# Late heads: the load of turned probabilities moves from SyncE's queue to ScalarE's, and the load of queries and keys moves behind the store

## The chip, the cores and the metric

The kernel runs on one core of one Trainium2 chip. The metric is the device time of one execution in microseconds (us). The time before is the median of three executions.

## The reference

The reference is causal attention with a forgetting gate on 4 x 8 heads, 576 positions and 64 features per head, followed by two pairs of dense layers on 2304 tokens:

```
scores = q @ k.T / 8 + cum[:, None] - cum[None, :]     # cum = cumsum(log f), causal mask
attn   = exp(scores - rowmax) / rowsum;  x = attn @ v   # heads side by side: [2304, 512]
h = relu(x @ w_in);   x = (h * h) @ w_out              # 512 -> 2048 -> 512
h = x @ w2_in;  y = (h - tanh(h)) @ w2_out             # 512 -> 2048 -> 512
```

All of it is float32. The kernel computes a float32 product from rounded halves: each operand is split into a rounded part and a rest, and three products are summed.

## The kernel before, in words

**Three kinds of work on one TensorE.** The attention of the 32 heads and the first dense pair run interleaved. The first pair (phase 1) works on eight blocks of 288 tokens. For each block and each of 16 slices `i` of the 2048 hidden units, `h_step` makes 12 matmuls (tile `hp`, line 138), ScalarE applies relu and the square (lines 148 to 150), an engine makes the rest `gl` (line 101), and two slices later `y_step` makes 12 matmuls (tile `yp`, line 164). In the stretch spoken of here `hp` has a single PSUM bank, so the next 12 `hp` matmuls wait until ScalarE's relu (line 148) has read the bank. The second pair (phase 2) follows when all heads are done. PSUM banks for attention come from one pool of three.

**Heads 16 to 31, the late heads.** `attention_late` handles head `k` in five steps. `scores(k, t)` makes the five score tiles: matmuls into `s_ps` (lines 476, 477), row minimum on VectorE (443), exponential on ScalarE (452), normalisation (463). `turn(t)` transposes the tile in 32 x 32 pieces on VectorE into the single tile `T` (lines 503, 506, 509). When all five are turned, `put(k)` stores `T` (1 MB) to memory (`p_d<-T`, line 512), and `get(k)` loads it back in four pieces in an order that completes the transposition (`PTl<-p_d`, line 518). `PTl` and `PTh` are single tiles. `split_p` makes the rounded half `PTh` on GpSimd (recorded at line 90 of a helper) and the rest `PTl` on VectorE (line 101), in four chunks. `pv(k)` multiplies with the values (tile `o_ps`, lines 549, 552, 554); its first matmul needs the first chunk of `PTh`. The result's upper half is evicted from PSUM by ScalarE as `xt` (the call of `rounded` in `pv`, recorded at line 88), and VectorE adds it to the lower half. Every second head stores the pair's output (`x_d<-xsh`, `x_d<-xs`).

Since `PTl` is a single tile, `get(k)` has to wait until the last matmul of `pv(k-1)` has read it, and it has to wait until the store `put(k)` has landed. In the program `get(k)` stands at the end of the step, behind `pv(k-1)`.

`load(k+2)` loads the queries and keys of the head after next into the single tile `R` (576 KB, line 225) and four rows into `QB` (line 227); `prep` splits `R` into `QA` and `QB` on ScalarE, VectorE and GpSimd one step later. In the program `load(k+2)` stands ahead of the second half of `split_p`.

**Who issues and in which order.** Before, SyncE's queue issues all loads and stores (`ENG["put"]` and `ENG["get"]` are `"S"`). An engine runs its instructions in a fixed order, and an instruction that waits holds up all behind it. The first two blocks keep the order of the program text. From the third block on a list scheduler places the instructions of every engine by its own estimates of time, within the dependencies. `tc.issue_after(ins)` adds one: what is issued inside it on the engine of `ins` comes behind `ins`. So a small change in the text gives another order on all engines.

In the rows and the text a head's load is called early when the head's last turn stands, in VectorE's order, ahead of the split of the head before; it is called late when that turn stands behind the split.

Of the kernel before, what the change touches and what calls it, by code (L numbers as in the profile page):

```python
# [16 lines left out]
B, H, S, D = 4, 8, 576, 64  # L17
NU = B * H
# [15 lines left out]
ENDS = (28, 27, 27, 27, 32, 24)  # L34
ENG = {
# [18 lines left out]
def kernel(  # L54
# [25 lines left out]
    def pre(u):  # L80
        return "" if u < UT else "l_"

    def by(name):
        return {"A": nc.scalar, "V": nc.vector, "P": nc.gpsimd, "S": nc.sync}[ENG[name]]

    def rounded(eng, out, in_):
        if eng is nc.scalar:
            eng.activation(out, in_, AF.Copy)  # L88
        elif eng is nc.gpsimd:
            eng.tensor_scalar(out, in_, 1.0, 1.0, ALU.mult, ALU.mult)  # L90
        else:
            eng.tensor_copy(out, in_)
# [80 lines left out]
    psa = att.enter_context(tc.tile_pool(name="psa", bufs=3, space=bass.MemoryType.PSUM))  # L173

    STORED = set()
    R, QA, QB, VR, VH, ST, XS, P, PT = {}, {}, {}, {}, {}, {}, {}, {}, {}

    def latest(engine):
        return next(x for x in reversed(nc.cur_bb.bb.instructions) if x.engine == engine)
# [43 lines left out]
    def load(u):  # L223
        R[u] = one.tile([128, 2, S], F32, tag="R", name="R")
        nc.sync.dma_start(R[u], qk[u])
        QB[u] = two.tile([68, 2, S], F32R, tag="QB", name="QB")
        nc.sync.dma_start(QB[u][64:68].bitcast(F32), aug_d[u])
# [7 lines left out]
    def prep(u):  # L235
        r = R.pop(u)
        qa = two.tile([128, 2, S], F32R, tag="QA", name="QA")
        QA[u] = qa
        split_qk(r, qa, QB[u], *(pre(u) + x for x in ("qb_q", "qa_lo", "qb_lo")))
        ST[u] = two.tile([128, 4, 6], F32, tag="ST", name="ST")  # L240
        by(pre(u) + "st").memset(ST[u], 1.0)

    def load_v(u):
        VR[u] = two.tile([128, 5, D], F32, tag="VR", bufs=2, name="VR")
        nc.sync.dma_start(VR[u], v[u])
# [183 lines left out]
    def store_x(b, pair, xs, c0, c1):  # L429
        STORED.add((b, pair, c1))  # L430
        n = c1 - c0
        xh = one.tile([128, S], F32R, tag="xsh", name="xsh")
        rounded(by(pre(b * H) + "xh"), xh[:, :n], xs[:, c0:c1])
        rest(by(pre(b * H) + "xl"), xs[:, c0:c1], xs[:, c0:c1], xh[:, :n])
        nc.sync.dma_start(x_d[b][pair][:, 0, c0:c1], xh[:, :n].bitcast(F32))
        nc.sync.dma_start(x_d[b][pair][:, 1, c0:c1], xs[:, c0:c1])
# [28 lines left out]
    def bank(u, name):  # L465
        return psa.tile([128, 512], F32, tag="at", name=name)

    def scores(u, t):
        qa, qb, st = QA[u], QB[u], ST[u]
        n, q0 = NKEY[t], Q0[t]  # L470
        rows = 64 if t == 0 else 128
        cuts = [(0, 320), (320, 576)] if t == 4 else [(0, n)]
        mn = None
        for i, (a, b) in enumerate(cuts):
            ps = bank(u, "s_ps")
            nc.tensor.matmul(ps[:, :b - a], qa[:, 0, q0:q0 + 128], qa[:, 1, a:b], start=True, stop=False)  # L476
            nc.tensor.matmul(ps[:, :b - a], qb[:, 0, q0:q0 + 128], qb[:, 1, a:b], start=False, stop=True)  # L477
            mn = row_min(P[t], ps, st, t, i, a, b, mn)
        soften(P[t], st, t, mn, f"{pre(u)}n{t}")
# [20 lines left out]
    def turn(t):  # L500
        p, T = P[t], PT["t"]
        if t == 0:
            nc.vector.transpose(T[0:64, 0:2, 3, 0], p[0:64, :64].rearrange("p (b j) -> p b j", b=2))
            return
        nch = min(t + 1, 4)
        nc.vector.transpose(T[:, :, :nch, t - 1].rearrange("p b a j -> p a b j"),
                            p[:, :nch * 128].rearrange("p (a b j) -> p a b j", a=nch, b=4))
        if t == 4:
            nc.vector.transpose(T[:, 0:2, 2, 0], p[:, 512:576].rearrange("p (b j) -> p b j", b=2))

    def put(u):
        by("put").dma_start(p_d[u % 2], PT["t"].rearrange("p b a s j -> p (b a s j)"))

    def get(u):
        src = p_d[u % 2].rearrange("(q i) (b n) -> i q b n", q=4, b=4)
        for b in range(4):
            dst = PT["l"][32 * b:32 * b + 32].rearrange("p q a s j -> p q (a s j)")
            by("get").dma_start(dst.bitcast(F32), src[:, :, b])  # L518
# [8 lines left out]
    def pv(u):  # L527
        vh, vr = VH.pop(u), VR.pop(u)
        b, h = divmod(u, H)
        e = h % 2  # L530
        ps = bank(u, "o_ps")
        if u < UT:
            hi, lo = (PT[k].rearrange("p q a s j -> p (q a s j)").rearrange("p (c t j) -> p c t j", c=4, t=4) for k in "hl")
            po = ps.rearrange("p (s j) -> p s j", s=4)
            at = lambda p, c, t: p[:, c, t:]
            po4, p4 = ps[0:64, 384:512].rearrange("p (q j) -> p q j", q=4), PT["t"][0:64, :, 3, 1]
            po_at = lambda t: po[:, t:]
            p0 = PT["t"][0:64, 2:4, 3, 0]
        else:
            hi, lo = PT["h"], PT["l"]  # L540
            po = ps.rearrange("p (q s j) -> p q s j", q=4, s=4)
            at = lambda p, c, t: p[:, :, c, t:]
            po4, p4 = po[0:64, :, 3], lo[0:64, :, 2, 0].bitcast(F32)
            po_at = lambda t: po[:, :, t:]
            p0 = lo[0:64, 0:2, 3, 0].bitcast(F32)
        seq = [(hi, 0), (hi, 1), (lo, 1), (hi, 2), (lo, 2), (hi, 3), (lo, 3), (None, 4), (lo, 0)]
        for n, (pt, c) in enumerate(seq):
            if pt is None:
                nc.tensor.matmul(po4, vr[0:64, 4], p4, start=False, stop=False)
                continue  # L550
            t = max(0, c - 1)
            nc.tensor.matmul(po_at(t), vh[:, c].rearrange("p a d -> p (a d)"), at(pt, c, t), start=(n == 0), stop=(n == 8))  # L552
        ps0 = bank(u, "o0_ps")
        nc.tensor.matmul(ps0[0:64, 0:64], vr[0:64, 0], p0, start=True, stop=True)
        if e == 0:
            XS[0] = two.tile([128, S], F32, tag="xs", name="xs")
        xs = XS[0]
        r = slice(64 * e, 64 * e + 64)
        xt = one.tile([64, 512], F32, tag="xsh", name="xt")
        rounded(nc.scalar, xt, ps[64:128])  # L560
        if u < UT:
            nc.vector.tensor_tensor(xs[r, 64:], ps[0:64], xt, ALU.add)
        else:
            nc.vector.tensor_tensor(
                xs[r, 64:].rearrange("p (s q j) -> p q s j", s=4, q=4),
                ps[0:64].rearrange("p (q s j) -> p q s j", q=4, s=4),
                xt.rearrange("p (q s j) -> p q s j", q=4, s=4), ALU.add,
            )
        rounded(by(pre(u) + "xs0"), xs[r, 0:64], ps0[0:64, 0:64])
        if e == 1:  # L570
            store_x(b, h // 2, xs, 0, S)
# [42 lines left out]
    def attention_late():  # L614
        for k in range(UT + 1, NU + 1):
            now = k < NU
            if now:
                load_v(k)
                scores(k, 4)
            yield  # L620
            if now:
                scores(k, 3)
                turn(4)
            yield
            if k + 1 < NU:
                prep(k + 1)
            prep_v(k - 1)
            split_p(0)
            if now:
                scores(k, 2)  # L630
                turn(3)
            yield
            if k + 2 < NU:
                load(k + 2)
            split_p(1)
            if now:
                scores(k, 1)
                scores(k, 0)
                turn(2)
            yield  # L640
            if now:
                turn(1)
                turn(0)
                put(k)
            pv(k - 1)
            yield
            if now:
                get(k)

    X = {0: [f1.tile([128, NK, TB], F32R, tag="xhl", bufs=4, name="xhl") for _ in range(2)]}  # L650
    setup()
# [221 lines left out]
```

## Time and profile before

| | |
|---|---|
| median of 3 executions | 1088.86 us (1084.09 to 1089.58) |
| profiled execution | 1081.43 us, span 1079.7 us |
| mean granted TensorE clock | 0.987 |
| TensorE busy | 1029.2 us, 95% of the span |
| VectorE, ScalarE, GpSimd busy | 594.0, 524.7, 250.6 us |
| DMA | 134.83 MB, 38.9% of the engines' span on one queue |
| late heads, from the first store to the last output | about 255 to 550 us of the span |

TensorE is PE in the rows, its weight loads are PEld, VectorE is DVE, ScalarE is ACT, GpSimd is POOL, SyncE is SP; a q behind the name (SPq) is the engine's queue of issued transfers. A row with `[2.17 <-POOL PTh L90]` says that the engine sat idle for 2.17 us before the instruction and that the split on GpSimd ended this. The granted clock is the share of TensorE's full 2.4 GHz; the lower level is 1.2 GHz.

### The profile page before, as it was taken

Reading aid. Unit: us, or ns where it says so; the run is one execution under the profiler, and the core shown is the slowest. Engines: PE = TensorE matmul, PEld = TensorE weight load, DVE = VectorE, ACT = ScalarE, POOL = GpSimd, SP = SyncE. Lnnn points to the kernel's source line nnn. Section 1 sums busy time; section 2 is a strip of 40 time slices with the busy share of each in tenths; the row PEclk is TensorE's granted clock in tenths of the full one; section 3 lists DMA queues with packets and bytes.
Section 4 is the critical chain, followed back from the end, with each engine's and each line's share of the span. In section 5 each row is a group of like instructions: output and inputs, shape, how many; then the busy total and the mean of one; then the engine's idle time right before and its main releaser. Section 6 shows DMA issues by size and latency. Waiting matters only on the chain.

```text
span 1079.7 us, 16821 instructions
## 1 busy us (share of the span) xinstructions
PE 1029.2 (95%) x6048; PEld 898.8 (83%) x6048; DVE 594.0 (55%) x1566; ACT 524.7 (49%) x1221; POOL 250.6 (23%) x358
## 2 busy tenths in 40 slices
PE   4899999999999898999999999999999999999998
PEld 3577678888998888888889999888888888888898
DVE  5887777768787767877525545642222322222232
ACT  6977677665556446455436667432222222222232
POOL 4244455555353442534210000000000000000000
PEclk9989999999999899999989999999999999999999
DMA  7657643225955658745646088100200300110010
GB/s 243 199 138 213 185 140 136 89 82 174 293 180 171 195 154 253 258 141 162 184 161 228 2 305 285 45 1 25 92 1 1 117 1 1 39 40 1 1 40 21
DMA packets 63301, 134.83 MB, mean 125 GB/s; under 512 B 6416, under 2 KB 31568, under 8 KB 61168
## 3 DMA queue, kind: packets, MB, share of 16 engines
q1 hardware_dynamic: 63216, 133.74, 38.9%
q8 instruction: 48, 0.79, 0.3%
q14 instruction: 37, 0.30, 0.1%
HBM read 93.94 MB, written 39.78 MB: 124 GB/s over the span
## 4 chain that ended last, share of the span: by engine, by line
PE 75%; DMA 11%; DVE 6%; POOL 2%; issue 2%; SPq 2%; ACT 2%; POOLq 0%; ACTq 0%; DVEq 0%
PE hp L138 32%; PE yp L164 32%; DMA PTl<-p_d 6%; PE o_ps L552 3%; DMA p_d<-T 3%; PE o_ps L367 2%; DVE PTl L101 2%; PE s_ps L476 1%; SPq L518 1%; DVE P L443 1%; PE s_ps L477 1%; DMA raw<-in_w_dram 1%; POOL PTh L90 1%; PE s_ps L326 1%; PE t_ps L487 1%
## 5 line engine op out<-in xcount | busy, mean ns | idle before, releaser
L138 PE MATMUL hp<-xhl,w 128*128 128x288 f32 (+2 forms) x2496 | 454.2, 329 | 2.5 <-ACT tmp L148 1.7
L138 PEld LDWEIGHTS hp<-xhl,w 128*128 128x128 f32 x2496 | 388.8, 192 | 41.0 <-issue 2.7
L164 PE MATMUL yp<-ghl,w 128*128 128x512 f32 (+1 forms) x960 | 216.0, 374 | 0.0
L164 PE MATMUL yp<-gh,w 128*128 128x288 f32 x1024 | 200.9, 301 | 0.0
L164 PEld LDWEIGHTS yp<-ghl,w 128*128 128x128 f32 x960 | 168.4, 188 | 34.5
L153 DVE TENSOR_TENSOR tmp<-hp,tmp 128x512 f32<-128x512 f32 (+1 forms) x80 | 51.0, 638 | 209.8 <-ACT tmp L152 209.8
L164 PEld LDWEIGHTS yp<-gh,w 128*128 128x128 f32 x1024 | 161.9, 191 | 1.6 <-issue 0.4
L152 ACT ACTIVATE tmp<-hp 128x512 f32<-128x512 f32 (+1 forms) x80 | 44.4, 555 | 225.0 <-PE hp L138 224.8
L164 PE MATMUL yp<-gl,w 128*128 128x288 f32 x512 | 133.5, 299 | 2.6 <-DVE gl L101 1.5
L148 ACT ACTIVATE tmp<-hp 128x288 f32<-128x288 f32 x128 | 51.9, 407 | 121.6 <-PE hp L138 118.4
L452 ACT ACTIVATE P<-P,ST 128x320 f32<-128x320 f32 (+4 forms) x151 | 84.6, 561 | 39.5 <-DVE ST L443 38.2
L164 PEld LDWEIGHTS yp<-gl,w 128*128 128x128 f32 x512 | 90.4, 190 | 5.0 <-DVE gl L101 2.3
L463 POOL TENSOR_SCALAR P<-P,ST 128x448 f32<-128x448 f32 (+4 forms) x88 | 58.4, 666 | 93.3 <-DVE ST L457 52.3
L101 DVE TENSOR_TENSOR ghl<-tmp,ghl 128x512 fp32r<-128x512 f32 (+1 forms) x80 | 51.1, 639 | 49.2 <-ACT ghl L88 49.2
L443 DVE CUSTOM_DVE_ANT_0 P<-s_ps,mk 128x320 f32<-128x320 f32 (+3 forms) x151 | 63.6, 433 | 25.2 <-PE s_ps L477 12.0
L101 DVE TENSOR_TENSOR gl<-tmp,gh 128x288 fp32r<-128x288 f32 x96 | 48.4, 505 | 47.2 <-ACT tmp L150 46.6
L101 DVE TENSOR_TENSOR PTl<-PTl,PTh 128x512 fp32r<-128x512 f32 (+1 forms) x64 | 51.9, 841 | 39.4 <-POOL PTh L90 39.3
L88 ACT ACTIVATE ghl<-tmp 128x512 fp32r<-128x512 f32 (+1 forms) x80 | 47.2, 590 | 49.9 <-DVE tmp L153 49.8
L101 DVE TENSOR_TENSOR w<-wst,w 128x512 fp32r<-128x512 f32 x64 | 46.1, 725 | 28.9 <-ACT w L88 28.6
L90 POOL TENSOR_SCALAR PTh<-PTl 128x512 fp32r<-128x512 f32 (+1 forms) x64 | 46.3, 750 | 59.8 <-DMA PTl<-p_d 59.0
L149 ACT ACTIVATE gh<-tmp 128x288 fp32r<-128x288 f32 x128 | 56.5, 443 | 4.1 <-PE yp L164 1.2
L150 ACT ACTIVATE tmp<-tmp 128x288 f32<-128x288 f32 x128 | 56.0, 438 | 2.1
(122 smaller groups left out, 1187.7 us busy)
## 6 DMA issues: line engine op xcount, KB each, us to landing
raw<-in_w_dram SPq DMA_DIRECT2D x64, 512.0 KB
p_d<-T SPq DMA_DIRECT2D x16, 1024.0 KB
PTl<-p_d SPq DMA_DIRECT2D x64, 256.0 KB
R<-in_qk_dram SPq DMA_DIRECT2D x24, 576.0 KB
xhl<-y_d SPq DMA_DIRECT2D x16, 512.0 KB
xhl<-x_d SPq DMA_DIRECT2D x14, 576.0 KB
y_d<-yst SPq DMA_DIRECT2D x14, 576.0 KB
VR<-in_v_dram SPq DMA_DIRECT2D x32, 160.0 KB
```

The source lines that it names most:

```text
L88: eng.activation(out, in_, AF.Copy)
L90: eng.tensor_scalar(out, in_, 1.0, 1.0, ALU.mult, ALU.mult)
L101: eng.tensor_tensor(out, in_, hi.bitcast(F32), ALU.subtract)
L138: nc.tensor.matmul(ps, w[:, k * 128:(k + 1) * 128], xk, start=(jj == 0), stop=(jj == 11))
L148: nc.scalar.activation(tmp, ps, AF.Relu)
L149: nc.scalar.activation(gh, tmp, AF.Square)
L150: nc.scalar.activation(tmp, tmp, AF.Square)
L153: nc.vector.tensor_tensor(tmp, ps, tmp, ALU.subtract)
L164: nc.tensor.matmul(yp[m][:, :n], w[:, c], x, start=(i == 0 and j == 0), stop=(i == NF - 1 and j == 2))
L443: nc.vector.tensor_tensor_reduce(p[:rows, a:b], ps[:rows, :b - a], mk[:rows, o:o + b - a], -0.125, 3.0e38 if mn is None else mn, ALU.add, ...
L452: nc.scalar.activation(p[:rows, :n], p[:rows, :n], AF.Exp, bias=mn, scale=-1.0, accum_out=st[:rows, 1, t:t + 1])
L463: by(n_by).tensor_scalar(p[:rows, :n], p[:rows, :n], st[:rows, 3, t:t + 1], 1.0, ALU.mult, ALU.mult)
```

## The change

`get` is issued from ScalarE. In `attention_late` it is issued within the step, behind the eviction `xt` of `pv(k-1)`, which the new dictionary `XT` remembers. `load(k+2)` moves from ahead of `split_p(1)` to behind `put(k)`, and is tied behind it on SyncE. The load of head 16, which stands in `attention`, changes its engine alone.

```diff
-    "w1_lo0": "V", "w1_lo1": "V", "w2_lo0": "V", "w2_lo1": "V", "sq": "V", "w1_sh": "V", "w2_sh": "V", "gl7": "V", "put": "S", "get": "S", "xld": "S", "wld": "S", "gl": "P", "qb_q": "A", "qa_lo": "V", "qb_lo": "P", "vh": "V", "vl": "V",
+    "w1_lo0": "V", "w1_lo1": "V", "w2_lo0": "V", "w2_lo1": "V", "sq": "V", "w1_sh": "V", "w2_sh": "V", "gl7": "V", "put": "S", "get": "A", "xld": "S", "wld": "S", "gl": "P", "qb_q": "A", "qa_lo": "V", "qb_lo": "P", "vh": "V", "vl": "V",
@@ -558,6 +558,7 @@
         xt = one.tile([64, 512], F32, tag="xsh", name="xt")
         rounded(nc.scalar, xt, ps[64:128])
+        XT[0] = latest(EngineType.Activation)
@@ -630,8 +631,6 @@
             yield
-            if k + 2 < NU:
-                load(k + 2)
             split_p(1)
@@ -642,10 +641,14 @@
                 put(k)
+                if k + 2 < NU:
+                    with tc.issue_after(latest(EngineType.SP)):
+                        load(k + 2)
             pv(k - 1)
+            if now:
+                with tc.issue_after(XT[0]):
+                    get(k)
             yield
-            if now:
-                get(k)
```

**The load's place.** On SyncE before, from the store of head 25 (`p_d_72`) to the load of head 26 (`p_d_71`); the pieces of `get` stand behind the store and behind `VR`, the values of a later head:

```order
L512 DMA p_d_72<-T 128x2048
L245 DMA VR<-in_v_dram 128x320
L518 DMA PTl<-p_d_72 32x4x512 x4
L227 DMA QB<-aug_d 4x1152
L713 DMA y_d<-yst 128x4x288 x2
L737 DMA xhl<-x_d_69 128x4x288
L225 DMA R<-in_qk_dram 128x1152
L737 DMA xhl<-x_d_69 128x4x288
L245 DMA VR<-in_v_dram 128x320
L512 DMA p_d_71<-T 128x2048
L435 DMA x_d_70<-xsh 128x576
L436 DMA x_d_70<-xs 128x576
```

On SyncE now, the same two stores:

```order
L512 DMA p_d_72<-T 128x2048
L225 DMA R<-in_qk_dram 128x1152
L227 DMA QB<-aug_d 4x1152
L245 DMA VR<-in_v_dram 128x320
L716 DMA y_d<-yst 128x4x288 x2
L740 DMA xhl<-x_d_69 128x4x288 x2
L245 DMA VR<-in_v_dram 128x320
L512 DMA p_d_71<-T 128x2048
L225 DMA R<-in_qk_dram 128x1152
L227 DMA QB<-aug_d 4x1152
```

On ScalarE now, behind the eviction of head 25's output, with the late load of head 26; `QA<-R` is the first step of `prep`:

```order
L88 ACTIVATE xt<-o_ps 64x512
L88 ACTIVATE VH<-VR 128x4x64
L88 ACTIVATE xsh<-xs 128x576
L148 ACTIVATE tmp<-hp 128x288
L149 ACTIVATE gh<-tmp 128x288
L150 ACTIVATE tmp<-tmp 128x288
L452 ACTIVATE P_1553,ST<-P_1553,ST 128x576
L452 ACTIVATE P_1551,ST<-P_1551,ST 128x448
L518 DMA PTl<-p_d_71 32x4x512 x2
L148 ACTIVATE tmp<-hp 128x288
L518 DMA PTl<-p_d_71 32x4x512
L149 ACTIVATE gh<-tmp 128x288
```

SyncE no longer issues the pieces; the store is followed at once by `R`. On ScalarE a late load stands several instructions behind the eviction. An early load, as that of head 25, stands directly behind it:

```order
L88 ACTIVATE QA<-R 128x1152
L88 ACTIVATE xt<-o_ps 64x512
L518 DMA PTl<-p_d_72 32x4x512 x4
L148 ACTIVATE tmp<-hp 128x288
L452 ACTIVATE P_1553,ST<-P_1553,ST 128x576
L452 ACTIVATE P_1551,ST<-P_1551,ST 128x448
```

So a wait of these four pieces holds up the relu (line 148) and the exponentials (452) behind them.

**VectorE around the split of head 19.** Before, the last turn of head 20 (`T<-P_1547`) stands behind the four chunks of the split (`PTl<-PTl,PTh`):

```order
L503 STREAM_TRANSPOSE T<-P_1546 64x2x32
L101 TENSOR_TENSOR gl<-tmp,gh 128x288
L101 TENSOR_TENSOR PTl<-PTl,PTh 128x4x128 x2
L101 TENSOR_TENSOR PTl<-PTl,PTh 128x4x96
L101 TENSOR_TENSOR PTl<-PTl,PTh 128x4x64
L506 STREAM_TRANSPOSE T<-P_1547 128x2x4x32
```

Now:

```order
L503 STREAM_TRANSPOSE T<-P_1546 64x2x32
L101 TENSOR_TENSOR gl<-tmp,gh 128x288
L506 STREAM_TRANSPOSE T<-P_1547 128x2x4x32
L101 TENSOR_TENSOR PTl<-PTl,PTh 128x4x128 x2
L101 TENSOR_TENSOR PTl<-PTl,PTh 128x4x96
L101 TENSOR_TENSOR gl<-tmp,gh 128x288
```

The last turn of head 20, and with it the store, moved ahead of the split of head 19.

**TensorE between the output of head 24 and that of head 25.** Before, from the last matmul of head 24's output to the first of head 25's there are 40 matmuls of the dense pair (between the two pieces shown stand 12 matmuls `yp` and five score matmuls):

```order
L552 MATMUL o_ps<-PTl,VH 128x512
L476 MATMUL s_ps<-QA 128x256
L477 MATMUL s_ps<-QB 128x256
L476 MATMUL s_ps<-QA 128x448
L477 MATMUL s_ps<-QB 128x448
L138 MATMUL hp<-xhl,w_0_455 128x288 x12
```

```order
L477 MATMUL s_ps<-QB 128x64
L138 MATMUL hp<-xhl,w_0_575 128x288 x12
L164 MATMUL yp<-gh,w_1_462 128x288 x4
L552 MATMUL o_ps<-PTh,VH 128x512
L554 MATMUL o_ps<-PTl,VR 64x64
```

Now the same stretch ends two matmuls earlier:

```order
L477 MATMUL s_ps<-QB 128x64
L138 MATMUL hp<-xhl,w_0_575 128x288 x12
L164 MATMUL yp<-gh,w_1_462 128x288 x2
L552 MATMUL o_ps<-PTh,VH 128x512 x2
L554 MATMUL o_ps<-PTl,VR 64x64
```

What TensorE has to do between the two outputs, its cover for the load, is nearly the same there.

## Rows read from the trace of the kernel before

**Rows 1.** Windows: length, busy us of each engine, granted clock, DMA share, GB/s.
```profile
250.00:550.00 300.00, 277.16 (x1848) 257.62 (x1848) 221.06 (x659) 156.04 (x403) 128.99 (x165) 0.97 0.64 195
...
550.00:600.00 50.00, 50.00 (x378) 50.00 (x377) 20.17 (x41) 30.71 (x70) 1.43 (x1) 1.00 0.60 209
```

**Rows 2.** Waits of the whole span: us in total, times, longest.
```profile
PE o_ps L552 <- POOL PTh L90: 17.6, 9, 4.1
```

**Rows 3.** Timeline of TensorE: start, us, instruction, idle time before it.
```profile
355.87 0.80 PE L552 MATMUL o_ps<-PTh,VH 128*128 128x512 f32 x1 [4.08 <-POOL PTh L90]
...
432.17 0.50 PE L552 MATMUL o_ps<-PTh,VH 128*128 128x512 f32 x1 [1.70 <-POOL PTh L90]
...
455.05 0.49 PE L552 MATMUL o_ps<-PTh,VH 128*128 128x512 f32 x1 [1.35 <-POOL PTh L90]
...
541.96 0.79 PE L552 MATMUL o_ps<-PTh,VH 128*128 128x512 f32 x1 [3.79 <-POOL PTh L90]
```

**Rows 4.** Windows of 10 us in which the granted clock fell.
```profile
330.00:340.00 10.00, 7.83 (x43) 7.15 (x42) 6.67 (x14) 3.36 (x13) 5.44 (x6) 0.83 0.39 110
...
350.00:360.00 10.00, 5.92 (x29) 5.10 (x28) 4.59 (x13) 2.75 (x10) 4.80 (x6) 0.79 0.73 203
360.00:370.00 10.00, 10.00 (x62) 9.56 (x62) 8.33 (x25) 4.95 (x11) 4.66 (x6) 0.87 0.57 207
...
470.00:480.00 10.00, 9.16 (x50) 8.21 (x50) 9.74 (x28) 3.43 (x10) 6.17 (x9) 0.83 0.23 75
...
540.00:550.00 10.00, 8.04 (x37) 6.99 (x38) 4.04 (x7) 1.30 (x3) 2.91 (x4) 0.66 0.01 3
```

**Rows 5.** Timeline of SyncE's queue, heads 16, 25 and 26.
```profile
255.37 0.33 SPq L512 DMA_DIRECT2D p_d<-T  x1
...
259.33 1.78 SPq L518 DMA_DIRECT2D PTl<-p_d  x4
...
423.87 1.74 SPq L518 DMA_DIRECT2D PTl<-p_d  x4
...
440.87 0.33 SPq L512 DMA_DIRECT2D p_d<-T  x1
...
445.82 1.74 SPq L518 DMA_DIRECT2D PTl<-p_d  x4
...
451.73 0.35 SPq L225 DMA_DIRECT2D R<-in_qk_dram  x1
```

**Rows 6.** Timeline of GpSimd, the splits of heads 25 and 26.
```profile
431.50 2.91 POOL L90 TENSOR_SCALAR PTh<-PTl 128x512 fp32r<-128x512 f32 x4 [3.39 <-DMA PTl<-p_d]
...
454.38 2.92 POOL L90 TENSOR_SCALAR PTh<-PTl 128x512 fp32r<-128x512 f32 x4 [2.67 <-DMA PTl<-p_d]
```

**Rows 7.** Timeline of ScalarE, the evictions of heads 24's and 25's outputs.
```profile
423.85 0.59 ACT L88 ACTIVATE xt<-o_ps 64x512 f32<-64x512 f32 x1 [1.19 <-PE o_ps L552]
...
439.02 0.59 ACT L88 ACTIVATE xt<-o_ps 64x512 f32<-64x512 f32 x1 [1.31 <-PE o_ps L552]
```

**Rows 8.** Waits of SyncE's queue, 250 to 550 us.
```profile
SPq L225 <- DVE QA L101: 41.6, 13, 7.9
...
SPq L518 <- DMA p_d<-T: 20.5, 12, 4.9
...
SPq L512 <- DVE T L503: 13.7, 6, 7.7
```

**Rows 9.** The chain that ended last: start, us, what.
```profile
300.86 1.60 PE hp L138 x12
```

**Rows 10.** Timelines of SyncE and GpSimd, heads 17 and 30.
```profile
275.54 1.75 SPq L518 DMA_DIRECT2D PTl<-p_d  x4
...
284.38 2.91 POOL L90 TENSOR_SCALAR PTh<-PTl 128x512 fp32r<-128x512 f32 x4 [1.05 <-DMA PTl<-p_d]
...
518.91 1.77 SPq L518 DMA_DIRECT2D PTl<-p_d  x4
...
526.51 2.92 POOL L90 TENSOR_SCALAR PTh<-PTl 128x512 fp32r<-128x512 f32 x4 [3.68 <-DMA PTl<-p_d]
```

More of the change, by code (lines that the diff above doesn't have):

```diff
@@ L175 @@
     STORED = set()
-    R, QA, QB, VR, VH, ST, XS, P, PT = {}, {}, {}, {}, {}, {}, {}, {}, {}
+    R, QA, QB, VR, VH, ST, XS, P, PT, XT = {}, {}, {}, {}, {}, {}, {}, {}, {}, {}
     def latest(engine):
```

## The prediction

> **What bounds the kernel now.** I read the windows first. From 250 to 550 us, where the late heads run, TensorE works 277.16 of 300 us, so it is idle for 22.8 us; in the next 50 us, without heads, it has no idle time [rows 1]. The waits come next: nine times, for 17.6 us in all, TensorE waits at the first output matmul of a head for GpSimd's split [rows 2], and the split waits for the load `PTl<-p_d` [rows 6]. The timeline gives the nine waits head by head: 0.37 us at head 19, 2.17 at 20, 4.08 at 21, 1.73 at 23, 1.70 at 25, 1.35 at 26, 0.65 at 27, 1.80 at 29 and 3.79 at 31 [rows 3] (four of the nine, the last among them). Behind the larger ones the granted clock falls: 0.83, 0.79, 0.87, 0.83 and 0.66 in windows of 10 us, so TensorE loses 1.7 + 2.1 + 1.3 + 1.7 + 3.4 = 10.2 us of full speed there [rows 4]. About 33 us is the most that can be won. The bound of this stretch is a chain that goes around once per head: output of the head before, load, split, output; in a late head (as the text ahead uses the word) the store stands in it too.
>
> **The two kinds of head.** Head 25 is an early one. The output of head 24 is done at 423.85, where its eviction starts [rows 7]. SyncE issues the load at 423.87, and this takes 1.74 us for four pieces [rows 5]. The split starts at 431.50 [rows 6], the output matmul at 432.17 [rows 3]. So the chain from output to output takes 8.3 us, of which SyncE's queue cost 0.02. Head 26 is a late one: the store is issued at 440.87, the load 4.95 later at 445.82 [rows 5], the split follows 8.56 after that [rows 6], and TensorE starts at 455.05 [rows 3].
>
> **What SyncE's queue costs now.** It stands 41.6 us at the load of `R` until VectorE is done with the head before, and 13.7 us at the store until VectorE has turned the last tile [rows 8]. The second wait says that the store is reached before its data is there, so the first held nothing up in those cases. The load waits 20.5 us for the store [rows 8], which the change doesn't shorten. In the heads looked at SyncE was ready when the data was. What the change takes off this queue was therefore hardly on the path.
>
> **The Trainium skill on this.** The page "DMA: Bandwidth & Descriptors", section "Rules for kernel authors", says that spreading transfers over several issuing queues brings no bandwidth, as all run on the same 16 engines, and saves issue time alone. The trace agrees as far as it can: the 1.74 us of issue move to another engine, they do not vanish. By that rule rival C below gains nothing from its own queue, and the sum stays as it is; without the rule C's price stands.
>
> **The terms.** One: the early loads. ScalarE may issue only behind the eviction, 0.59 us [rows 7], where SyncE issued at its start: +0.57 us per head. In the new order the early heads with a short gap are 18, 20, 25, 27, 29 and 31. Between the output of the head before and their own TensorE has 47, 40, 38, 44, 38 and 60 matmuls of the dense pair. Twelve take 1.60 us [rows 9], so 0.133 each, and the scores add some 1.2 us (none at 31): 7.4, 6.5, 6.3, 7.0, 6.3 and 8.0 us of cover. Against 8.3 + 0.57 = 8.87 they wait 1.5 + 2.4 + 2.6 + 1.9 + 2.6 + 0.9 = 11.9 us. Other work on ScalarE can make it more; bounds 0 and one more activation of 0.59 each.
>
> Two: the late heads, in the new order 19, 21, 23, 24, 26, 28 and 30 (head 16 is the first and has no split before it); before, 19, 20, 21, 22, 24, 26, 28 and 30 were. Head 26 needed 16.0 us from the eviction at 439.02 [rows 7] to its first output matmul at 455.05 [rows 3], with its store 1.8 us behind the eviction, at 440.87 [rows 5]; with the store at the eviction it is 14.2. Cover in the new order is 11.3 us at 19, 9.2 at 23, 14.9, 14.1, 15.6, 13.7 and 15.6 at the others. Waits: 2.9 at 19, 5.0 at 23, and some 0.5 each at 24, 26, 28 and 30, in all 9.9. The two heads with little cover are what the new order does worst; that 20 and 22 become early is what it does best.
>
> Three: ScalarE's place for a late load. It stands several activations behind the eviction, by the scheduler's estimate of the store. If ScalarE gets there late, the load is late; if early, ScalarE stands. Bounds: none, and 4.9 us per head, the longest such wait of SyncE [rows 8]. I take none for the chain, since the order puts some eight activations in between and those fill most of the store's time.
>
> Four: ScalarE's issue time, 64 pieces at 1.74 / 4 = 0.43 us, 28 us in a stretch where it works 156 of 300 [rows 1]. Bounds: nothing, and all 28 us. I take nothing, nearest to the row that TensorE's idle time ends at the output matmul: a relu delayed by 1.74 us stands beside the 1.60 us of `yp` matmuls, and what TensorE loses ahead of an output matmul at which it waits anyway it does not lose twice.
>
> Five: `R` behind the store. `R` now moves beside a late load. Loads with little beside them reach the split 7.60 us after their issue (518.91 to 526.51), with others beside 8.84 (275.54 to 284.38) [rows 10]. Head 26 at 8.56 already has `R` beside it, issued at 451.73 [rows 5]. Bounds per late head -0.96 (as if the other queue spared it) and +1.24. I take nothing more on the chain of 14.2, which holds 0.96 of it.
>
> Six: the rest. The other idle time, 22.8 - 17.6 = 5.2 us, and the clock's 10.2 us I leave as they are: the new waits over 2 us are about as many (19, 20, 23, 25, 29).
>
> **The sum.** New waits 11.9 + 9.9 = 21.8 us against 17.6: +4.2 us. The profiled execution takes 1081.43 us (span 1079.7), so 1085.6 on it. It lies 7.4 us under the median of the runs shown, 1088.86, and the change is put on that: 1093.1, rounded to 1093.
>
> **The rivals.** B, ScalarE stands at the load. In a late head it waits for the store and then issues for 1.74 us, with the relu behind it; with one `hp` bank TensorE stops once wait and issue exceed the 1.60 us of `yp`. A wait of 1.5 us makes 1.5 + 1.74 - 1.60 = 1.6 us of stop in each of 7 heads, 11 us on top of the forecast: 1104. For it: the four pieces stand directly ahead of relu and exponentials, and a store took 4.95 us at head 26, but its time is the scheduler's guess. Against it: part of the stop falls ahead of an output wait. If half of the stop falls there, it passes 5.4 us in all from a wait of some 0.2 us per late head.
>
> C, a queue of its own. The load no longer queues behind what SyncE issued. A late load wins 0.96 to 1.24 us, by term five. A store took 3.96 us at head 16 (255.37 to 259.33) and 4.95 at head 26 [rows 5]; no longer behind `R` it wins half of this, 0.5. Seven heads win about 11 us: 1093 - 11 = 1082. For it: the spread of 7.60 and 8.84 [rows 10]. Against it: `R` was issued before the store at head 16 too, and half of the heads are early. The skill's same page, section "Queues, rings and completion order", says that an engine takes turns between the queues that have work; by that the load would share instead of standing behind, which is this rival. No run here shows two queues side by side.
>
> D, the path isn't touched: early loads lose 0.57, late ones win about the same, and the order's shuffle cancels. Then 1089 within a few us. For it: about as many short covers before (56, 45, 40, 48, 40 and 48 matmuls at 20, 23, 25, 27, 29 and 31) as now.
>
> **How the numbers follow.** A change of 0.5%, 5.4 us, is about what a measurement of this kernel tells from none. The forecast has 0.42, with 1087 to 1099 as its own range: 0.30 of it within 0.5% and 0.12 above. B has 0.24, all slower. C has 0.16, all faster. D has 0.18: 0.12 within, 0.06 faster. That makes faster 0.22, same 0.42, slower 0.36. The range takes in C and B without their ends: 1077 to 1110.
>
> **What would show it.** Right: in the profile after, the load's first piece starts 0.6 us behind the start of `xt` in the early heads; TensorE's waits at `o_ps` sum to 20 to 24 us, the longest at 23 or 19; SyncE's waits for the store are gone and stand at ScalarE's queue. Term three is wrong if ScalarE waits over 1 us at line 518 in most late heads; four, if TensorE's idle time before `hp` for line 148, next to none now, grows to several us; five, if late loads take under 7.6 or over 9 us to the split. The whole is wrong if TensorE's idle time in the stretch falls under 18 us or passes 32.

## The result, and the profile after

The changed kernel takes 1092.63 us (median of 19 executions, 1089.6 to 1098.6) against 1086.09 us for the kernel before in the same runs (19 executions, 1081.05 to 1091.41). The ratio is 1.0065, 95% interval 1.0046 to 1.0084: slower by some 7 us. The profiled execution has a span of 1091.5 us and a mean granted clock of 0.984 (before: 1079.7 us, 0.987). The execution profiled before lay 4.7 us under its median, so the two traces stand further apart than the medians.

The stretch of the late heads, in windows of the changed kernel; the columns are the window, its length, TensorE's busy time with its matmuls, the granted clock, the DMA share and GB/s:

```profile
250.00:550.00 300.00, 270.79 (x1791) 0.95 0.63 191
550.00:600.00 50.00, 49.52 (x360) 1.00 0.68 231
```

TensorE is idle for 29.2 us where it was idle for 22.8 [rows 1], 6.4 us more, at a clock of 0.95 where it had 0.97. What it waits for from 250 to 560 us (us in total, times, longest):

```profile
PE o_ps L552 <- POOL VH L101: 9.9, 2, 5.1
PE yp L164 <- DVE gl L101: 5.5, 1, 5.5
PE o_ps L552 <- POOL PTh L90: 4.8, 5, 1.6
PE hp L138 <- ACT tmp L148: 4.2, 4, 1.5
```

The wait for the split, 17.6 us before [rows 2], is down to 4.8. In part the change relieved the chain that the prediction followed, in part other waits now cover it: with these taken out (run 1) it is 10.1. In its place stand 15.4 us, where the kernel before had 1.5 us for a `gl`: two waits for `VH`, the rounded values that the output matmul takes as weights, and one for `gl`, a rest of the dense pair. With the 4.2 us for the relu that is 15.4 + 4.2 - 12.8 = 6.8 us, close to the 6.4 of the windows.

One of the two waits for `VH` stands at head 25. GpSimd there, before and after (start, us, instruction, idle time before it):

```profile
424.84 0.74 POOL L101 TENSOR_TENSOR VH<-VR,VH 128x256 fp32r<-128x256 f32 x1 [6.75 <-ACT VH L88]
```

```profile
439.17 2.47 POOL L90 TENSOR_SCALAR PTh<-PTl 128x512 fp32r<-128x512 f32 x4 [5.22 <-DMA PTl<-p_d]
441.62 1.21 POOL L101 TENSOR_TENSOR VH<-VR,VH 128x256 fp32r<-128x256 f32 x1
```

Before, GpSimd made the low part of `VH` at 424.84, ahead of the split at 431.50 [rows 6]. Now it stands 5.22 us at the split for the load and makes `VH` behind it. So the output starts not 0.7 us behind the split's start, as before, but 3.7 us behind it:

```profile
442.88 1.22 PE L552 MATMUL o_ps<-PTh,VH 128*128 128x512 f32 x2 [5.09 <-POOL VH L101]
...
522.39 1.22 PE L552 MATMUL o_ps<-PTh,VH 128*128 128x512 f32 x2 [4.80 <-POOL VH L101]
```

In the kernel before, `VH` stands ahead of its own split at all of the heads 17 to 31. Now it stands behind it at 22, 25 and 29. At head 22 VectorE's order has the same flaw: `gl`, whose inputs ScalarE had finished by 377.1, stands behind the split.

```profile
377.04 1.09 DVE L101 TENSOR_TENSOR PTl<-PTl,PTh 128x512 fp32r<-128x512 f32 x1 [2.78 <-POOL PTh L90]
...
381.74 1.53 DVE L101 TENSOR_TENSOR gl<-tmp,gh 128x288 fp32r<-128x288 f32 x1
```

```profile
383.33 1.33 PE L164 MATMUL yp<-gl,w 128*128 128x288 f32 x4 [5.54 <-DVE gl L101]
```

### The profile page after: what moved, and what is told of

Read it like the earlier page. It is cut to its first block, busy times and chain, and to the rows that moved or that the text cites. A ratio compares the mean times of both kernels' runs of the same rounds, so it can differ in the third digit from the quotient of the medians.

```text
span 1091.5 us, 16854 instructions
## 1 busy us (share of the span) xinstructions
PE 1032.5 (95%) x6048; PEld 900.0 (82%) x6048; DVE 587.9 (54%) x1566; ACT 525.6 (48%) x1221; POOL 250.4 (23%) x358
## 4 chain that ended last, share of the span: by engine, by line
PE 71%; DMA 13%; DVE 8%; ACT 3%; issue 2%; POOL 1%; ACTq 1%; SPq 1%; POOLq 0%; DVEq 0%
PE yp L164 31%; PE hp L138 30%; DMA PTl<-p_d 6%; DMA R<-in_qk_dram 4%; PE o_ps L552 2%; PE o_ps L367 2%; DMA raw<-in_w_dram 2%; DVE P L443 1%; PE s_ps L476 1%; PE s_ps L477 1%; DVE QA L101 1%; DMA p_d<-T 1%; DVE PTl L101 1%; PE t_ps L487 1%; DMA VR<-in_v_dram 1%
## 5 line engine op out<-in xcount | busy, mean ns | idle before, releaser
L164 PE MATMUL yp<-gh,w 128*128 128x288 f32 x1024 | 203.2, 303 | 2.2 <-ACT gh L149 1.5
L101 DVE TENSOR_TENSOR PTl<-PTl,PTh 128x512 fp32r<-128x512 f32 (+1 forms) x64 | 48.7, 788 | 28.6 <-POOL PTh L90 28.5
```

The lines of the kernel that those rows point to most:

```text
L101: eng.tensor_tensor(out, in_, hi.bitcast(F32), ALU.subtract)
L164: nc.tensor.matmul(yp[m][:, :n], w[:, c], x, start=(i == 0 and j == 0), stop=(i == NF - 1 and j == 2))
```

## The experiments

Three theories on the 7 us. ORDER: the scheduler, given other dependencies, put `VH` and `gl` behind the split, and nothing else is lost. R: the keys and queries, now loaded behind the store, land late; ScalarE waits 8.3 us at `QA` for them, seven times, and GpSimd waits for `QA`. QUEUE (RELU in the later runs): ScalarE's issuing of the load and its standing for the store hold up the relu.

A change of the text reorders all engines, so two kernels differ in more than the edit. Most of the kernels below therefore take the finished schedule of the changed kernel (or of the kernel before), fix it on every engine, and move single instructions in it. `insert` puts the named instructions into an engine's list; with no such line the lists are those of the original, row for row. The code shown is cut: lines that find the names, and those that take an instruction out of its old place, are left out.

**1. VH and gl back ahead of the split.**

```diff
+ for u in (22, 25, 29):
+     insert(POOL, [vh[u]], before=pth[4 * (u - 16)])     # first chunk of the own split
+ insert(DVE, gls, before=ptl[4 * (22 - 16)])             # the two gl that follow it
```

> The changed kernel with its order fixed on every engine, and two kinds of instruction moved back: VH's low part on GpSimd ahead of the head's own split at heads 22, 25 and 29, and two gl on VectorE ahead of head 22's split. Theory ORDER (the loss lies in what the new order put behind the split): the output of 25 and 29 starts 3.0 us sooner each, and the yp matmuls at head 22 some 5.1 us sooner, about 11 us in all, so 1081 to 1084 us, ratio to before 0.995 to 0.999. Theory R (the late load of R holds ScalarE and then GpSimd): under 3 us of this come back, ratio 1.004 to 1.0075. Theory QUEUE (ScalarE's issuing of the load costs): no change, 1.0065.

Measured: 1085.77 us, ratio to before 1.0004 (0.9989 to 1.0018). The loss is gone; the ratio had been 1.0065.

```profile
250.00:550.00 300.00, 278.14 (x1842) 0.97 0.66 195
```

```profile
PE o_ps L552 <- POOL PTh L90: 10.1, 10, 2.1
PE hp L138 <- ACT tmp L148: 4.9, 5, 2.4
```

The waits for `VH` are gone, idle time and clock are those of before (21.9 us, 0.97). Some of it has turned into waits for the split: 10.1 us where there were 4.8. So 6.8 us come back of the 11 expected, and the ratio lies just above ORDER's range and well below the other two.

**2. VH alone.** The first two lines of the edit above.

> The changed kernel with its order fixed, VH's low part ahead of the split at heads 22, 25 and 29 and gl left where it is: splits the 6.8 us that both together brought back. Theory ORDER: 25 and 29 bring 3 us each, head 22 nothing without gl: ratio 1.000 to 1.003. Rival: gl alone carried it, ratio 1.005 to 1.0075.

Measured: 1087.93 us, ratio 1.0027 (1.001 to 1.0044). `VH` brings 0.0038, about 4 us, `gl` the other 0.0023; the intervals overlap a little. The wait for `gl` is still there in the trace (5.4 us, once), the one for `VH` is gone.

**3. The same as a rule in the text.** The scheduler is free again, but for one rule.

```diff
             prep_v(k - 1)
-            split_p(0)
+            low = latest(EngineType.Pool)
+            with tc.issue_after(low):
+                split_p(0)
...
-            split_p(1)
+            with tc.issue_after(low):
+                split_p(1)
```

> The changed kernel with one rule more: GpSimd may issue the split of a head only behind the low part of that head's VH; the scheduler orders all the rest anew. Theory ORDER: TensorE's waits for VH (9.9 us) are gone, 5 to 8 us come back, ratio 0.998 to 1.002. Rival: VH behind the split was only where a late head happened to show, and the waits move to the split: ratio 1.004 or more.

Measured: 1087.01 us, ratio 1.0006 (0.9987 to 1.0024). That is in ORDER's range. The rule names GpSimd alone, but the scheduler's new order differs elsewhere too: in the order of VectorE in this kernel's trace, which is used for the order alone, the two `gl` stand ahead of head 22's split again. So the run shows that a rule in the text repairs the order; it does not tell `VH` from `gl`, as run 2 does.

**4. Theory R: the queries ahead of the store again.**

```diff
+ for u, names in loads.items():                           # R and QB of heads 19 to 31
+     insert(SP, names, before=puts[u - 2])
```

> The changed kernel with its order fixed, and R and QB of the second next head moved ahead of the store in SyncE's queue, nothing else. Theory R: ScalarE's waits at QA for R (8.3 us, 7 times) and for QB (2.5 us) fall below 2 us together, and 4 to 8 us come back: ratio 0.999 to 1.003. Theory ORDER: the waits at QA fall too, but the time moves by under 2 us: 1.005 to 1.008. Theory QUEUE: no change, 1.0065.

Measured: 1107.34 us, ratio 1.0211 (1.0187 to 1.0235), some 15 us slower than the changed kernel and outside every range. ScalarE's waits at `QA` for `R` are gone from the trace, as theory R wants, and the time went the other way. Since the edit costs in other places, it is run 1 that speaks against R: there `R` stays late, and the loss is gone all the same. Two things happen here. One is at the store. Head 19 in the changed kernel's queues of SyncE and ScalarE:

```profile
313.81 0.32 SPq L512 DMA_DIRECT2D p_d<-T  x1
314.18 0.42 SPq L225 DMA_DIRECT2D R<-in_qk_dram  x1
```

```profile
318.62 1.85 ACTq L518 DMA_DIRECT2D PTl<-p_d  x4
```

and those of this kernel:

```profile
318.37 0.38 SPq L225 DMA_DIRECT2D R<-in_qk_dram  x1
318.84 0.28 SPq L227 DMA_DIRECT2D QB<-aug_d  x1
319.23 0.33 SPq L512 DMA_DIRECT2D p_d<-T  x1
```

```profile
325.65 1.76 ACTq L518 DMA_DIRECT2D PTl<-p_d  x4
327.45 1.17 ACT L88 ACTIVATE QA<-R 128x1152 fp32r<-128x1152 f32 x1 [4.09 <-issue]
```

From the store's issue to the load's it takes 6.42 us with `R` 0.9 us ahead of the store, 4.81 with `R` behind it; at heads 24 and 28, with `R` 1.2 and 1.0 us ahead, it is 7.76 and 6.14 against 4.92 and 5.02. At heads 21 and 26, where `R` went out 2.3 and 2.0 us ahead of the store, next to nothing is lost: 4.98 and 4.75 against 4.74 and 4.99. ScalarE, in whose order the load stands, does nothing meanwhile: 4.09 us idle ahead of `QA` at head 19, of which it issues for 1.76.

The other is at the load. At heads 16 and 17 SyncE comes to `R` just as ScalarE issues the load. From load to split it takes 12.2 and 12.7 us, against 8.3 and 11.1 in the changed kernel, and TensorE waits at both, where it had not waited at all:

```profile
274.82 0.80 PE L552 MATMUL o_ps<-PTh,VH 128*128 128x512 f32 x1 [3.65 <-POOL PTh L90]
...
298.89 0.49 PE L552 MATMUL o_ps<-PTh,VH 128*128 128x512 f32 x1 [2.71 <-POOL PTh L90]
```

So at the store of head 19 this kernel is already 5.4 us late. In all, TensorE's waits for the split rise from 4.8 to 11.9 us, those for the relu from 4.2 to 7.8. `R` close ahead of the store or beside the load is costly in this order. But the kernel before had it in neither place at its late heads: there `R` went out 2.0 to 6.2 us ahead of the store, and from the store's issue to the load's it took 3.9 to 5.6 us. So this run puts `R` into a third place; it does not undo a part of the change.

**5. Theory QUEUE in the new order: the load back on SyncE.**

```diff
+ ENG["get"] = "S"
+ for k, names in gets.items():
+     insert(SP, names, after=loads[k + 2][1])             # behind put(k), R, QB; without R behind the store: behind put(k)
```

> The changed kernel with its order fixed, the four pieces PTl<-p_d issued from SyncE behind QB of the same head instead of from ScalarE. Theory QUEUE: ScalarE is rid of 28 us of issuing and of standing at the store, 5 us or more come back: ratio 1.002 or less. Theories ORDER and R: ratio 1.004 to 1.010; R and QB are issued in the same place, and the early heads lose nothing, since SyncE stands free by then.

Measured: 1097.51 us, ratio 1.0109 (1.0084 to 1.0133): 4.9 us slower than the changed kernel (the intervals just touch), against QUEUE and just beyond the range of the others. TensorE has two new waits, the first at 271.50:

```profile
PE hp L138 <- DMA xhl<-x_d: 4.6, 1, 4.6
PE s_ps L476 <- DVE xs L565: 4.4, 1, 4.4
```

SyncE stands at the load until the store has landed, 61.5 us at the 16 heads, and the next block's input `xhl` stands behind it: issued at 267.00 instead of 262.13. So in this order ScalarE's queue is a gain too, by what SyncE can issue meanwhile.

**6. The load on ScalarE in the order of before.**

```diff
+ ENG["get"] = "A"
+ past = (4, 2, 3, 3, 5, 9, 7, 0, 8, 0, 9, 0, 7, 0, 7, 3)
+ for k, names in gets.items():                            # activations past xt of head k-1
+     insert(ACT, names, after=free[free.index(xts[k - 9]) + past[k - 16]])
```

> The kernel before with its order fixed, the four pieces PTl<-p_d issued from ScalarE, behind as many activations past xt as had been done when SyncE issued them (4, 2, 3, 3, 5, 9, 7, 0, 8, 0, 9, 0, 7, 0, 7, 3 at heads 16 to 31). Theory QUEUE: 3 to 7 us slower, ratio 1.003 to 1.0065. Theories ORDER and R: ratio 0.998 to 1.002.

Measured: 1101.57 us, ratio 1.0144 (1.0118 to 1.0169), 16 us slower than before and more than any theory had. The same move of the load that gains 4.9 us in one order loses 16 in the other. TensorE's wait for the relu, next to none before, is 8.0 us in this stretch. The rest begins at head 16, where the output is 8.7 us late (276.59 against 267.91). 3.0 us of this the trace has at the store already, ahead of anything that the edit moved; 5.7 come between store and output:

```profile
258.33 0.33 SPq L512 DMA_DIRECT2D p_d<-T  x1
...
262.99 1.48 SPq L737 DMA_DIRECT2D xhl<-x_d  x2
```

```profile
264.39 0.41 ACT L148 ACTIVATE tmp<-hp 128x288 f32<-128x288 f32 x1 [1.95 <-PE hp L138]
264.83 0.45 ACT L149 ACTIVATE gh<-tmp 128x288 fp32r<-128x288 f32 x1
264.84 1.81 ACTq L518 DMA_DIRECT2D PTl<-p_d  x4
```

```profile
275.92 1.20 POOL L90 TENSOR_SCALAR PTh<-PTl 128x512 fp32r<-128x512 f32 x2 [3.52 <-DMA PTl<-p_d]
```

Two things add up. The load comes 6.51 us behind the store instead of 3.96 [rows 5], since it now stands behind a relu that itself waits for TensorE. And `xhl`, 1.15 MB in two transfers, stood behind the load on SyncE; now it goes out 1.85 us ahead of it, and from the load to the split it takes 11.08 us instead of 7.90.

**7. The same, with xhl held back.**

```diff
+ for n in xhl_of_heads_16_17_24:
+     add_dependency(n, gets[k][3])                        # waits until the load has landed
```

> As the kernel before with its order fixed and the load on ScalarE (ratio 1.0144), and in addition the three pairs of xhl<-x_d near heads 16, 17 and 24 wait until the load of that head has landed, as they stood behind it in SyncE's queue before. Theory CONTENTION (the bulk loads that SyncE now issues ahead of the load share the DMA engines with it): issue to split at heads 16 and 24 falls from 11.1 and 11.7 us to about 8, 6 us or more come back, ratio 1.005 to 1.009. Theory RELU (ScalarE's issuing and standing holds up the relu): under 2 us come back, ratio 1.012 or more.

Measured: 1095.64 us, ratio 1.0095 (1.0067 to 1.0124). From load to split head 16 now takes 8.96 us (257.88 to 266.84) and head 24 8.06 (it had 11.73), and 0.0049, about 5 us, come back (the intervals overlap a little). That is under the 6 expected, and the ratio just outside the range; but it is more than the 2 us that RELU allowed. So the transfers that overtook the load are about a third of the 16 us; the wait for the relu (7.1 us still) and the later places of the load are left.

**8. The same hold in the new order.** The edit of 7 on top of the edit of 1.

> As the changed kernel with VH and gl moved ahead of the split (ratio 1.0004), and in addition the three pairs of xhl<-x_d wait for the load of heads 16, 17 and 24. Theory CONTENTION: issue to split falls from 9.8, 9.9 and 9.2 us to about 8 at these three heads, 2 to 5 us come back, ratio 0.996 to 0.999. Theory RELU: no gain; the new block's hp waits for xhl, ratio 1.000 to 1.004.

Measured: 1097.21 us, ratio 1.0109 (1.0077 to 1.014), a miss on both sides. The load gets faster (head 16: 7.5 us instead of 9.8), but `xhl` is needed: TensorE waits 5.8 us for it, and SyncE stands 27.4 us at the three places with all that is behind.

**9. The relu ahead of QA.**

```diff
+ for u in (19, 23):
+     insert(ACT, [relu], before=qa)                       # both follow the load of head u
```

> As the changed kernel with VH and gl moved (ratio 1.0004), and at heads 19 and 23 the relu that stands behind the load, QA and an exponential on ScalarE moved to directly behind the load. TensorE waits 1.47 and 2.41 us for these two. Theory RELU (the load on ScalarE holds up the relu behind it, and TensorE with its one hp bank): 2 to 4 us come back, ratio 0.997 to 0.9985. Rival: the wait moves to the next output matmul of the head, ratio 0.9995 to 1.002.

Measured: 1086.81 us, ratio 1.0012 (0.9992 to 1.0031): nothing comes back, though the wait does go.

```profile
PE o_ps L552 <- POOL PTh L90: 12.8, 11, 2.1
...
PE hp L138 <- ACT tmp L148: 1.3, 4, 0.5
```

3.6 us less for the relu, 2.7 more for the split; the idle time is the same (21.7 against 21.9 us). The wait moved, as the rival said: with the load fixed in time, TensorE meets the same load later.

**10 and 11. Each part of the change alone,** the scheduler free.

```diff
  # 10: "get": "A", get(k) behind XT[0]; load(k + 2) ahead of split_p(1) as before
  # 11: "get": "S", get(k) at the end of the step as before; load(k + 2) tied behind put(k)
```

> One part of the change alone: the four pieces PTl<-p_d on ScalarE behind xt; R and QB are loaded where the kernel before loads them, and the scheduler orders the rest. VH stands ahead of the own split at all heads there, and R stands ahead of the store in SyncE's queue at 13 heads. Theory STORE (R in front of the store in SyncE's queue makes the store late, as in the run with 1.0211): ratio 1.006 to 1.02. Theory ORDER alone (what matters is VH behind the split): ratio 0.996 to 1.003.

> The other part of the change alone: R and QB loaded behind the store, the four pieces PTl<-p_d on SyncE as before; the scheduler orders the rest. VH stands ahead of the split at all heads. Theory STORE (a store that no longer queues behind R is the gain of the change): ratio 0.988 to 0.998. Rival (R lands later and holds up ScalarE at QA): ratio 1.002 to 1.010.

Measured: the pieces on ScalarE alone 1098.48 us, ratio 1.0114 (1.0086 to 1.0143); the queries behind the store alone 1084.40 us, ratio 0.9983 (0.9955 to 1.0011). The first is in STORE's range, but its rows don't bear STORE out: with `R` 4.6 to 7.2 us ahead of them, the late stores took 3.9 to 5.7 us to the load's issue, as in the kernel before (3.9 to 5.6). TensorE waits 21.8 us for the split and 6.5 for the relu. The longest wait, 6.64 us, is at head 21, where store and load took no longer than elsewhere; 4.52 is at head 24, where `xhl` was issued 4.1 and 0.4 us ahead of the load, and the load took 13.6 us to the split. As the scheduler placed everything anew, what makes this kernel slow is not shown. The second can't be told from no change, and is a miss; it was to be faster by 0.2 to 1.2%. Both parts together are better than the first alone. In both kernels `VH` stands ahead of its split at all heads: neither part alone brings the flaw.

**12. The queries behind the store in the order of before.**

```diff
+ for u, names in loads.items():
+     insert(SP, names, after=puts[u - 3])                 # the store that R stood ahead of
```

> The kernel before with its order fixed, and each R and QB that stood ahead of a store in SyncE's queue moved to directly behind that store, nothing else. Theory STORE: late stores land 0.5 to 1 us sooner in the eight late heads, ratio 0.993 to 0.998. Rival (R lands later, ScalarE stands at QA in an order that counted on it): ratio 1.002 to 1.010.

Measured: 1154.57 us, ratio 1.0645 (1.061 to 1.0681). The edit did more than was meant. `QB` had stood behind the load in this order, and with `R` it came ahead of it:

```profile
323.68 0.34 SPq L512 DMA_DIRECT2D p_d<-T  x1
324.12 0.37 SPq L225 DMA_DIRECT2D R<-in_qk_dram  x1
332.01 0.27 SPq L227 DMA_DIRECT2D QB<-aug_d  x1
332.33 0.33 SPq L245 DMA_DIRECT2D VR<-in_v_dram  x1
332.76 1.81 SPq L518 DMA_DIRECT2D PTl<-p_d  x4
```

SyncE stands at `QB` until TensorE has read the old one, 129.4 us in 13 waits at the late heads, with the load behind it; TensorE waits 66.8 us for the split. So this run says nothing on `R`. It shows what a wait ahead of the load costs on an in-order queue.

## Why the prediction was right or wrong

The time was right: 1093 forecast, 1092.63 measured. That the two meet to 0.4 us is luck: the forecast stands on a median of three executions, 1088.86, and the kernel before took 1086.09 in the 19; on that it would be 1090.3. The sign of the small difference was right, its size nearly: +4.2 us, against +6.5 us between the medians. But the way there was only half right, and this too is luck: two errors cancelled. The waits for the load were forecast at 21.8 us and came to 4.8; the other idle time was to stay at 5.2 us and came to 24.4.

Of its signs for the whole, one held: TensorE's idle time, 29.2 us, lies between 18 and 32. The waits at `o_ps` sum to 15.5 us up to 560 us (9.9 + 4.8 + 0.8), not 20 to 24, and the longest stand at 25 and 29, not at 23 or 19.

**Terms one and two** were too large: 21.8 us of waits at the first output matmul. What the load itself makes TensorE wait is 4.8 us, and 10.1 in run 1, where `VH` and `gl` no longer cover it. Term one failed in the step "ScalarE may issue only behind the eviction". At head 25 the load goes out ahead of the eviction's start, not 0.6 us behind it:

```profile
430.13 1.17 ACT L88 ACTIVATE QA<-R 128x1152 fp32r<-128x1152 f32 x1 [1.02 <-DMA R<-in_qk_dram]
431.13 0.31 ACTq L518 DMA_DIRECT2D PTl<-p_d  x1
431.32 0.59 ACT L88 ACTIVATE xt<-o_ps 64x512 f32<-64x512 f32 x1
```

Behind in the queue is not behind in time: the issue needs the reading of `PTl` to be done, not the eviction to have run. Of the six early heads 25 and 29 did wait, but for `VH`; 18, 20, 27 and 31 waited 1.0, 1.6, 1.1 and 0.5 us. In run 1 all six wait for the load, 7.3 us in all where 11.9 were forecast. In term two, head 19 waited 0.74 instead of 2.9 us and head 23 not at all. Its cover was counted in the order's matmuls alone: TensorE, held up by `gl` at head 22, let out that head's result only when the store of 23 was under way, so 23 ran as an early head. That is not all of it: in run 9, without the waits for this `gl` and the relu, head 23 waits 0.91 us, still not 5.0. And the four times 0.5 us of this term are an allowance: by the covers that it gives, only head 28 comes to that.

**Term six** was the step that failed on the other side: it left the other idle time, 5.2 us, as it was. It grew by 19.2 us, which the waits for `VH` and `gl` (15.4) and for the relu (4.2) account for. The prediction read how the order moved the turns against the splits, and did not read what else had moved behind the split on GpSimd and VectorE. Run 1 shows that this, and not the load, is the loss. The clock followed. In six windows of 50 us it was 1.00, 0.97, 0.93, 1.00, 0.97 and 0.93 before, which makes 10.0 us of full speed lost, an estimate; after, it makes 15.5:

```profile
250.00:300.00 50.00, 47.10 (x303) 0.93 0.73 226
300.00:350.00 50.00, 45.19 (x300) 0.97 0.56 160
350.00:400.00 50.00, 43.53 (x287) 0.93 0.68 206
400.00:450.00 50.00, 42.98 (x279) 0.93 0.65 199
450.00:500.00 50.00, 47.43 (x335) 1.00 0.66 194
500.00:550.00 50.00, 44.56 (x294) 0.93 0.52 162
```

**Terms three and four**, nothing for ScalarE's place and for its issuing. Three held: between the end of its last activation and the first piece of a late load ScalarE stands 1.23 us at head 28, 1.05 at 24 and 0.59 at 19, elsewhere next to nothing. Four was to be wrong if the idle time ahead of `hp` grew to several us, and it grew to 4.2. But run 9 takes most of a like wait away and gains nothing, so the time doesn't show it in this order. In the order of before neither term holds: the load came 2.5 us later at head 16, and the waits for the relu were 8.0 us (run 6). Rival B, ScalarE standing at the load, is real where the store is late: run 4.

**Term five**, nothing for `R` behind the store, holds by the rows. From the store's issue to the load's the late heads took 3.9 to 5.6 us before, 4.7 on the mean, and 4.7 to 5.0 now, 4.9 on the mean (without 23); from load to split the means are 7.9 and 8.4. That is some 0.7 us more per late head, within the bounds. By its sign, 7.6 to 9 us to the split, heads 24 with 9.72 and 30 with 7.45 fall out, five of seven don't. Its picture was off: `R` does not move beside a late load but ahead of it, issued 4.4 to 4.6 us earlier. What `R` costs in other places run 4 shows. The 0.5 us per store that rival C had the change win is not seen in these means.

Rival C also had the load gain by a queue of its own. The Trainium skill, page "DMA: Bandwidth & Descriptors", section "Queues, rings and completion order", has an engine take turns between the queues with work. Run 4 agrees: at head 16, from 266 to 268 us, `R` on SyncE's queue (q1) and the load on ScalarE's (q10) moved nearly as many packets (packets, MB, share of the engines' time). `R` has the larger packets, so the load got a third of the bytes.

```profile
q1 hardware_dynamic: 79, 0.36, 67.8%
q10 hardware_dynamic: 83, 0.16, 33.9%
```

Run 6 shows no turns: from 265 to 268 us `xhl`, issued 1.85 us ahead of the load, had the engines nearly to itself, though the load's issue began at 264.84. Whether the load's packets were ready by then the rows don't tell.

```profile
q1 hardware_dynamic: 967, 1.09, 104.2%
q10 hardware_dynamic: 3, 0.01, 1.9%
```

In both cases the load lost by the other queue, and what was a shelter on one queue is gone.

That none of the runs beats the kernel before beyond its interval stays the state of it: 0.9983 (run 11), 1.0004 and 1.0006. Why the scheduler put `VH` behind the split stays open; it does so with both parts of the change, and with neither alone (runs 10 and 11).

## What to carry to other kernels

Where a scheduler orders the work, read in the new order what has come to stand behind a waiting instruction on every engine, not only the instructions that the edit names; a small operation behind a waiting one can cost more than the transfer that was moved. To learn what an edit itself is worth, fix the order and move the single instruction: the same move of the load gained 5 us in one order and lost 16 in the other. And a queue that stands at a wait also holds back what would compete with the transfer waited for; before a load gets a queue of its own, list what will overtake it.

## What was not expected of the hardware

A transfer that stands behind activations on ScalarE's queue is issued beside them: at head 29 its first piece went out at 511.09, 1.0 us ahead of the start of the eviction (512.09) that it stands behind. A transfer that must wait for data holds up the activations behind it: at head 19 of run 4 ScalarE stood 2.3 us for the store and then 1.8 issuing. And 576 KB issued 0.9 us ahead of a 1 MB store on the same queue made the store's data available 1.6 us later at head 19, and at heads 21 and 26, 2.3 and 2.0 us ahead, next to nothing (4.98 and 4.75 us against 4.74 and 4.99). On this one queue the two ran one behind the other. A packet of `R` is a row of 4608 bytes, one of the store 8192. From 320 to 321.5 us and from 322.5 to 324:

```profile
DMA packets 71, 0.33 MB, mean 218 GB/s; under 512 B 0, under 2 KB 0, under 8 KB 71
...
DMA packets 78, 0.63 MB, mean 418 GB/s; under 512 B 1, under 2 KB 1, under 8 KB 2
```

In the first stretch all packets are `R`'s, in the second nearly all the store's.
